# Forgetting attention and a SiLU feed-forward on one core: the mask of two late score groups on VectorE, DMA transposes issued ahead of loads, and the attention outputs of the fourth quad transposed by DMA

## The chip, the core and the metric

The kernel runs on one core of one Trainium2 chip. The metric is the device time of the core in microseconds (us). Before the change the median of 3 runs is 344.74 us, the lowest 343.42 and the highest 345.34. The profile that is shown is of one execution, with a span of 342.4 us.

## What is computed

Batch 8, heads 8, sequence 576, head dimension 64. Each head has causal attention with a decay that comes from running sums of log f. The result, 4608 rows of 512, goes through a feed-forward layer of width 2048 with SiLU.

```python
scores = np.matmul(q, k.transpose(0, 1, 3, 2)) / np.sqrt(D)
cum = np.cumsum(np.log(np.clip(f, 0.0001, 1.0)), axis=-1)
decay = cum[:, :, :, None] - cum[:, :, None, :]
scores = np.where(causal, -1e9, scores + decay)
attn = exp(scores - max) / (sum + 1e-9)
x = np.matmul(attn, v)            # (B, H, S, D), then to rows (B*S, H*D)
h = x @ w_in                      # 512 -> 2048
out = (h / (1 + np.exp(-h))) @ w_out
```

## The kernel before

**Decay.** The factor of a row cancels between numerator and sum, so only exp(-cum) of the key's position is left. It is multiplied into v (and into a column of ones beside v that gives the sum) on GpSimd: `convert_v0` (L340) for the first 128 positions of a batch, `convert_v` (L413) for the others.

**First section: the heads of all batches.** The first 128 positions of each batch are worked on alone. `turn0` (L277) turns q and k on TensorE, `scores0` (L309) makes the scores of the batch's 8 heads and ScalarE takes exp of them into u (L326). `out0` (L349) multiplies with v and VectorE normalises to xq (L368, L374); `back0` (L382) transposes xq on TensorE (L389) and ScalarE copies it to the feed-forward's input x (L390). The causal mask is made in one of two ways. `ban0` (L297) puts -30000 into the score bank with two 512-column matmuls of a ready-made ban (L300), and the scores are added on top. `mask0` (L333) leaves the bank alone and multiplies u with a triangle after exp, on VectorE (L335). Before the change batches 0 to 5 have the ban, 6 and 7 the mask. Batches 4 and 5 are done in the first call of `two_more` (L805), 6 and 7 in the second.

**Second section: the other 448 positions.** A *unit* n is a pair of heads of one batch, 32 in all; a *quad* m is two units, 16 in all, numbered from 0, so that the quad with m = 3 is the fourth. The loop over quads (L874) issues `scores`, `prepare` and `attend` of both units, and `back` of the quad before. `load_qk` (L152) loads q and k of a unit by four transfers from SyncE's queue (SP), `load_tails` (L165) and `load_v` (L174) use the same queue. `cast_qk` (L394) casts to bf16 on GpSimd, which works in program order and also issues the stores of the results (L591). `transposes` (L423) then turns q and k of the unit by a DMA transpose, again issued by SP. SP issues in program order: a transpose that waits for its cast holds all that stands behind it. `prepare(n)` (L839) casts and transposes unit n + 2 and loads unit n + 4.

`back(m)` (L531) transposes the normalised output xr of a quad to x. For the quads in `BY_DMA` (L488), 4 to 14 before the change, SP issues two DMA transposes (L538 for the 384 columns, L542 for the tail of 64 rows); for the others TensorE makes seven transposes (L548) and VectorE copies them out (L551, L554).

**Feed-forward, as filler.** The columns of x form groups: group 0 holds the heads of batches 0 to 3, 1 and 2 those of 4, 5 and of 6, 7, then one group of 384 columns for each batch (3 for batch 0, 4 for batch 1, and so on), and two groups of tails. `m1_chunk` (L560) makes one 128-row tile of h for a group: four matmuls (L567), tanh on ScalarE (L575), and gt on VectorE (L576). `m2_part` (L594) makes a quarter of an output tile: four matmuls (L612). Each such piece is called an M1 or M2 step here. `fill(us, least)` (L698) issues steps into the instruction order between pieces of attention, for an estimated number of microseconds and at least `least` steps; what is left or owed is carried in `at["left"]`. When no step can be issued, that is set to 0. `wanted` (L641) decides whether M1 or M2 is next, so that a group's M1 keeps pace with the M2 of the group before; a group's M1 may be issued once `ready` holds the group, and M2 once `open2` is set. In the loop a batch's group becomes ready two slots after `back` of its second quad. All of this is decided when the program is built; on the chip the order is fixed.

**Buffers.** Score banks: two of 2 PSUM banks (`psc`). All other PSUM tiles (hp, po, tp, tx, dn) share four banks in turn (`pbig`). th has three buffers, qkT three, qf and kf four.

Of the kernel before, what the change touches and what calls it, by code (L numbers as in the profile page):

```python
# [18 lines left out]
def kernel(  # L19
# [17 lines left out]
    NP = H // 2  # L37
# [7 lines left out]
    NU = B * NP  # L45
    NQ = NU // 2
# [52 lines left out]
    def xg(g):  # L99
        if g not in xgs:  # L100
            tag, bufs = {4 * P: ("x4", 1), 2 * P: ("x2" if g < 3 else "xt", 2), RB: ("x3", 3)}[GW[g]]
            xgs[g] = xpool.tile([P, NCC, GW[g]], BF16, name=tag, tag=tag, bufs=bufs)
        return xgs[g]
# [45 lines left out]
    def head(p, i):  # L149
        return p // 2 * 4 + 2 * i + p % 2  # L150

    def load_qk(n):  # L152
        b, p = divmod(n, NP)
        ts = []
        for name, src in (("qf", q), ("kf", k)):
            t = stage.tile([P, NR, 2, D], FP32, name=name, tag=name, bufs=4)
            for i in range(2):
                nc.sync.dma_start(
                    out=t[:, :, i, :],
                    in_=src[b, head(p, i), P:SM, :].rearrange("(c p) d -> p c d", p=P),  # L160
                )
            ts.append(t)
        qst[n] = tuple(ts)
# [113 lines left out]
    def turn0(b, i):  # L277
        src = qk0[b]
        if i == 0:
            qT0[b] = qktp.tile([P, NP, P], BF16, name="qT0", tag="qT0", bufs=2)  # L280
        dst, evac = ((qT0[b], nc.scalar.copy), (kT0[b], nc.vector.tensor_copy))[i]
        tp = pbig.tile([P, NP, NRUN, RUN], FP32, name="tp", tag="big")
        for c in range(RUN):
            for j in range(2):
                nc.tensor.matmul(  # L285
                    tp[j * D : (j + 1) * D, :, :, c].rearrange("p a r -> p (a r)"),
                    lhsT=src[:, i, c * D : (c + 1) * D],
                    rhs=sel[:, j, :],
                    start=True,
                    stop=True,  # L290
                )
        evac(
            out=dst[:, :, :].rearrange("p a t -> p (a t)"),
            in_=tp[:, :, :, :].rearrange("p a r c -> p (a r c)"),
        )

    def ban0(b):  # L297
        sc = psc.tile([P, 2, NP, P], FP32, name="sc", tag="sc")
        for i in range(2):
            nc.tensor.matmul(  # L300
                sc[:, i, :, :].rearrange("p a t -> p (a t)"),
                lhsT=ident_bf[:, :],
                rhs=ban[:, :, :].rearrange("p a t -> p (a t)"),
                start=True,
                stop=False,
            )
        return sc

    def scores0(b, sc=None):  # L309
        t = qT0.pop(b)  # L310
        fresh = sc is None
        u = upool.tile([P, 2, NP, P], BF16, name="u", tag="u")
        u0[b] = u
        if fresh:
            sc = psc.tile([P, 2, NP, P], FP32, name="sc", tag="sc")
        for p in range(NP):
            for i in range(2):
                r = slice(i * D, (i + 1) * D)
                nc.tensor.matmul(  # L319
                    sc[:, i, p, :],  # L320
                    lhsT=kT0[b][r, p, :],
                    rhs=t[r, p, :],
                    start=fresh,
                    stop=fresh or p == NP - 1,
                )
        nc.scalar.activation(  # L326
            out=u[:, :, :, :].rearrange("p i a t -> p (i a t)"),
            in_=sc[:, :, :, :].rearrange("p i a t -> p (i a t)"),
            func=ACT.Exp,
            scale=scale,  # L330
        )

    def mask0(b):  # L333
        x = u0[b][:, :, :, :].rearrange("p i a t -> p (i a) t")
        nc.vector.tensor_tensor(  # L335
            out=x, in0=x, in1=tri[:, None, :].to_broadcast([P, H, P]), op=ALU.mult
        )
# [85 lines left out]
    def transposes(n):  # L423
        src = qbf.pop(n)
        t = qktp.tile([P, NX, P], BF16, name="qkT", tag="qkT")
        qkT[n] = t[:, :, :].rearrange("p x c -> p (x c)")
        nc.sync.dma_start_transpose(
            out=t[:, :, :], in_=src[:, :, :].rearrange("p x c -> p (x c)")
        )
# [55 lines left out]

    NGR = 2 * NR + 1

    BY_DMA = [2 * 2 <= m < NQ - 1 for m in range(NQ)]  # L488

    def attend(n):  # L490
        b, p = divmod(n, NP)
# [39 lines left out]
    def back(m):  # L531
# [4 lines left out]
        xt = xg(g)[:, c0 : c0 + 2, :].rearrange("p i t -> p (i t)")[:, t0 * P : (t0 + 1) * P]  # L536
        if BY_DMA[m]:
            nc.sync.dma_start_transpose(  # L538
# [117 lines left out]
    def step(force=0):  # L656

        a, c = at["m1"], at["m2"]
        want = wanted(a, c)
        if not want:  # L660
            return None
        g1 = M1[a][0] if a < len(M1) else NG
        g2 = M2[c][0] if c < len(M2) else NG
        can1 = g1 in ready and not (M1[a][1] == 0 and g1 > g2 + 1)
        can2 = open2["w"] and c < len(M2) and g2 < g1
        kind = force if (force == 1 and can1) or (force == 2 and can2) else want
        if kind == 1:
            if M1[a][1] == 0:
                begin[g1] = (0, c)
            m1_chunk(g1, M1[a][1])  # L670
            at["m1"] += 1
            t = 4 * (GW[g1] / 2.4 + 2.5)
        else:
            m2_part(*M2[c])
            at["m2"] += 1
            t = 4 * (DM / 2.4 + 2.5)
        return t
# [6 lines left out]
    def plan(us_):  # L684

        a, c, kinds = at["m1"], at["m2"], []
        while us_ > 0:
            k = wanted(a, c)
            if not k:
                break  # L690
            kinds.append(k)
            if k == 1 and M1[a][1] == 0:
                begin[M1[a][0]] = (0, c)
            us_ -= (4 * (GW[M1[a][0]] / 2.4 + 2.5) if k == 1 else 4 * (DM / 2.4 + 2.5)) / 1000
            a, c = a + (k == 1), c + (k == 2)
        return kinds

    def fill(us_, least=0, ends=(0, 0)):  # L698

        left = us_ + at["left"]  # L700
        kinds = plan(left)
        kinds += [0] * (least - len(kinds))
        if any(ends) and kinds:
            if 2 not in kinds:
                kinds[0] = 2
            n1, n2 = len(kinds) - kinds.count(2), kinds.count(2)
            e0 = 1 if ends[0] else 0
            e1 = 1 if ends[1] and n2 > e0 else 0
            inner = n2 - e0 - e1
            n = n1 + inner  # L710
            mid = [2 if (x + 1) * inner // n > x * inner // n else 1 for x in range(n)]
            if inner and mid[-1] == 2 and e1 and not e0:
                mid = mid[::-1]
            kinds = [2] * e0 + mid + [2] * e1
        for k in kinds:
            t = step(k)
            if t is None:
                at["left"] = 0.0
                return
            left -= t / 1000  # L720
        at["left"] = left
# [80 lines left out]
    for c in range(NM):  # L802
        convert_v(0, c)

    def two_more(b, banned):  # L805
        for x in range(2):
            turn0(b + x, 0)
            turn0(b + x, 1)
            fill(0.6, 1)
        for x in range(2):  # L810
            if banned:
                scores0(b + x, ban0(b + x))
            else:
                scores0(b + x)
                mask0(b + x)
            fill(0.6 if x == 0 else 2.0 if banned else 2.8, 1 if x == 0 else 2)
        out0(b)
        fill(0.6, 1)
        out0(b + 1)
        fill(0.8, 2)  # L820
        back0(b, on_act)
        fill(0.6, 1)
        back0(b + 1, on_act)
        fill(0.6, 1)

    fill(5.0)
    two_more(4, True)
    ready.add(1)
    fill(5.0)
    open2["w"] = True  # L830
    begin[M1[at["m1"]][0]] = (M1[at["m1"]][1], at["m2"])
    fill(6.0)
    two_more(6, False)
    ready.add(2)
    fill(3.2)

    def prepare(n):  # L839

        b, p = divmod(n, NP)
        if n > NP - 1 and n + 4 < NU:
            load_qk(n + 4)
        if 0 < n < NU - 2:
            cast_qk(n + 2)
            transposes(n + 2)
        if n < NP - 1:
            load_qk(n + 4)
        if b + 1 == B:
            return  # L850
        if p == 0 and b > 0:
            load_tails(b + 1)
        if b == 0 and p >= 2 or b > 0 and p == 1:
            for c in range(NM) if b > 0 else range(2 * (p - 2), 2 * (p - 1)):
                load_v(b + 1, c)
        if n == NP - 1:
            load_qk(n + 4)
        if p >= 2:
            for c in range(2 * (p - 2), 2 * (p - 1)) if b > 0 else range(NM * (p - 2)):
                convert_v(b + 1, c)  # L860
# [13 lines left out]
    for m in range(NQ):  # L874
        n = 2 * m
# [4 lines left out]
        if m > 0:  # L880
            back(m - 1)
            if m % 2 == 0:
                b = m // 2 - 1
# [50 lines left out]
```

The softmax here doesn't subtract the row's maximum and nothing guards it: scores larger than these inputs give would overflow.

## Time and profile before

| | us | share of the span |
|---|---|---|
| span of the profiled execution | 342.4 | |
| TensorE, hp (L567), all shapes, 704 recorded | 128.3 | |
| TensorE, po (L612), 592 | 145.2 | |
| ScalarE busy | 216.6 | 63% |
| VectorE busy | 182.0 | 53% |
| GpSimd busy | 129.7 | 38% |
| chain that ended last: TensorE | | 91% |
| chain: ScalarE / VectorE / issue | | 5% / 3% / 1% |
| SP's queue: share of the 16 DMA engines' time | | 52.8% |

A line of a group or of the timeline gives start and length in us, engine, line of the kernel, operation, the tile that is written and those that are read (out<-in), shape and count; in brackets is the idle time of the engine just before it and what ended it. Matmuls overlap, so the length of a row of them is more than the time until the next one starts; the distance of starts is what TensorE spends. PE is the matmul, PEld the load of weights, DVE VectorE, ACT ScalarE, POOL GpSimd, SPq SyncE's issue of transfers. Some records of matmuls are missing, so a count can be too small.

### The profile page before, as it was taken

What the parts mean: (1) busy time and instruction counts of PE and PEld (TensorE: products, weight loads), DVE (VectorE), ACT (ScalarE), POOL (GpSimd) and SP (SyncE); (2) the same over time, 40 slices, a digit from 0 to 9 for tenths busy, and PEclk for the clock granted to TensorE, in tenths of its full rate; (3) what the DMA queues carried; (4) which work ended last, traced back from release to release, by engine and by line L of the source; (5) the groups of instructions that cost most, each with busy time, mean ns of one, the idle gap of its engine ahead of it and who ended that gap; (6) DMA issues with size and microseconds to landing.
All of it is one profiled execution on the core that took longest, in us unless ns stands there. A gap on an engine that the chain in (4) does not pass through costs nothing.

```text
span 342.4 us, 8894 instructions
## 1 busy us (share of the span) xinstructions
PE 335.9 (98%) x3567; PEld 199.2 (58%) x3567; DVE 182.0 (53%) x389; ACT 216.6 (63%) x401; POOL 129.7 (38%) x227
## 2 busy tenths in 40 slices
PE   8999999999999999999999999999999999999995
PEld 3745656577656656566465666656656565555654
DVE  4766736467557466357445654555655464444330
ACT  5767645877687676857759677595685944454431
POOL 8995317734637254065128128208320000001011
PEclk9999999999999999999999999999999999999999
DMA  8999999999999997899987799789832010001012
GB/s 154 193 183 220 179 202 155 241 212 199 197 192 179 189 198 168 164 215 162 162 195 153 162 192 214 159 148 218 166 86 56 25 42 33 31 32 63 31 53 71
DMA packets 141497, 50.44 MB, mean 147 GB/s; under 512 B 132368, under 2 KB 138768, under 8 KB 141456
## 3 DMA queue, kind: packets, MB, share of 16 engines
q1 hardware_dynamic: 131440, 32.70, 52.8%
q0 software_dynamic: 9856, 17.04, 21.3%
q8 instruction: 28, 0.46, 0.6%
q10 hardware_dynamic: 160, 0.13, 0.2%
q14 instruction: 13, 0.11, 0.1%
HBM read 36.85 MB, written 9.44 MB: 135 GB/s over the span
## 4 chain that ended last, share of the span: by engine, by line
PE 91%; ACT 5%; DVE 3%; issue 1%
PE po L612 36%; PE hp L567 34%; PE sc L459 7%; PE dn L506 5%; PE dn L515 3%; PE tp L285 3%; ACT u L463 2%; ACT th L575 2%; PE wm L232 1%; DVE gt L576 1%; PE sc L300 1%; PE sc L319 1%; ACT x L390 1%; DVE xq L374 0%; DVE xr L524 0%
## 5 line engine op out<-in xcount | busy, mean ns | idle before, releaser
L576 DVE SCALAR_TENSOR_TENSOR gt<-th,hp 128x384 bf16<-128x384 bf16 (+2 forms) x208 | 105.4, 522 | 82.9 <-ACT th L575 79.5
L575 ACT ACTIVATE th<-hp 128x384 bf16<-128x384 f32 (+2 forms) x208 | 95.2, 479 | 84.7 <-PE hp L567 82.5
L612 PE MATMUL po<-w_out_bf,gt 128*128 128x512 bf16 (+1 forms) x592 | 145.2, 374 | 0.0
L567 PE MATMUL hp<-x,w_in_bf 128*128 128x384 bf16 (+2 forms) x704 | 128.3, 321 | 0.6 <-DVE xt L554 0.4
L567 PEld LDWEIGHTS <-w_in_bf 128*128 128x128 bf16 x832 | 79.9, 98 | 57.0 <-DVE xt L554 0.7
L463 ACT ACTIVATE u<-sc 128x1024 bf16<-128x1024 f32 (+1 forms) x96 | 75.2, 821 | 9.7 <-PE sc L459 9.7
L612 PEld LDWEIGHTS <-gt 128*128 128x128 bf16 x592 | 53.3, 98 | 47.9 <-issue 2.5
L591 POOL DMA_DIRECT2D out_dram<-osb x38 | 21.0, 552 | 142.3 <-ACT osb L622 100.3
L413 POOL TENSOR_TENSOR vp<-vf,w_bf 128x520 bf16<-128x520 f32 (+1 forms) x32 | 35.2, 1104 | 27.7 <-DMA vf<-in_v_dram 26.2
L622 ACT ACTIVATE osb<-po 128x512 f32<-128x512 f32 (+1 forms) x37 | 22.1, 597 | 18.9 <-PE po L612 18.9
L468 DVE TENSOR_TENSOR u<-u,tri 128x768 bf16<-128x768 bf16 x32 | 21.6, 676 | 19.8 <-ACT u L463 19.8
L459 PE MATMUL sc<-qkT 64*128 64x128 bf16 (+1 forms) x640 | 26.7, 207 | 0.3 <-ACT th L575 0.2
L399 POOL CAST qkb<-qf 128x384 bf16<-128x384 f32 x32 | 17.4, 543 | 24.4 <-DMA qf<-in_q_dram 23.8
L482 DVE TENSOR_TENSOR ut<-ut,trit 128x128 bf16<-128x128 bf16 x32 | 9.5, 297 | 32.2 <-ACT ut L475 32.2
L459 PEld LDWEIGHTS <-qkT 64*128 64x128 bf16 x640 | 18.3, 94 | 11.7 <-issue 9.5
L475 ACT ACTIVATE ut<-sc 128x640 bf16<-128x640 f32 x32 | 23.3, 728 | 0.0
L506 PEld LDWEIGHTS <-u 128*128 128x128 bf16 x576 | 20.8, 97 | 2.5
L506 PE MATMUL dn<-vp,u 128*128 128x65 bf16 x384 | 21.8, 193 | 0.0
L524 DVE TENSOR_TENSOR xr<-dn,rec 128x448 bf16<-128x448 f32 x32 | 20.0, 625 | 1.1
L506 PE MATMUL dn<-v,u 128*128 128x65 bf16 x192 | 19.8, 193 | 0.0
L399 POOL CAST qkb<-kf 128x384 bf16<-128x384 f32 x32 | 16.9, 527 | 2.6 <-DMA kf<-in_k_dram 2.4
L567 PE MATMUL hp<-xt,w_in_bf 128*128 128x256 bf16 x128 | 17.7, 273 | 0.0
(68 smaller groups left out, 206.0 us busy)
## 6 DMA issues: line engine op xcount, KB each, us to landing
out_dram<-osb POOLq DMA_DIRECT2D x32, 256.0 KB, 3.2
vf<-in_v_dram SPq DMA_DIRECT2D x26, 256.0 KB, 5.2
qf<-in_q_dram SPq DMA_DIRECT2D x64, 96.0 KB, 3.3
kf<-in_k_dram SPq DMA_DIRECT2D x64, 96.0 KB, 2.9
w_in_bf<-in_moe_w_in_dram POOLq DMA_DIRECT2D x4, 512.0 KB, 7.2
w_out_bf<-in_moe_w_out_dram POOLq DMA_DIRECT2D x4, 512.0 KB, 10.1
vf<-in_v_dram POOLq DMA_DIRECT2D x6, 256.0 KB, 10.4
qkb<-in_q_dram POOLq DMA_DIRECT2D x8, 128.0 KB, 5.2
```

Source lines behind the costliest of these rows:

```text
L399: nc.gpsimd.tensor_copy(out=t2[:, c0 : c0 + NR, :].rearrange("p c x -> p (c x)"), in_=t[:, :, :, :].rearrange("p c h d -> p (c h d)"),)
L413: nc.gpsimd.tensor_tensor(out=vbf[b][r, c, :, :], in0=vst[b][c][r, :, :], in1=w_bf[r, c + 1, b * H : (b + 1) * H, None].to_broadcast([n, H ...
L459: nc.tensor.matmul(sc[:, i, o : o + q1 - q0], lhsT=kt, rhs=t[r, q0:q1], start=True, stop=True)
L463: nc.scalar.activation(out=u[:, :, c * SM : c * SM + w], in_=sc[:, :, 0:w], func=ACT.Exp, scale=scale)
L468: nc.vector.tensor_tensor(out=x, in0=x, in1=tri[:, None, None, :].to_broadcast([P, 2, NR, P]), op=ALU.mult,)
L475: nc.scalar.activation(out=ut[:, :, 0:3:2, :].rearrange("p k i t -> p i k t"), in_=sc[:, :, T0 : T0 + (NM + 1) * ST].rearrange("p i (k t) ...
L506: nc.tensor.matmul(dn[:, i * NR + c - 1, :], lhsT=u[:, i, o : o + P], rhs=vals(kb, i), start=(kb == 0), stop=(kb == c),)
L567: nc.tensor.matmul(hp[:, :], lhsT=w_in_bf[:, cc, fc * P : (fc + 1) * P], rhs=xcols(g, cc), start=(cc == 0), stop=(cc == NCC - 1),)
L575: nc.scalar.activation(out=th[:, :], in_=hp[:, :], func=ACT.Tanh, scale=0.5)
L576: nc.vector.scalar_tensor_tensor(out=gt[:, fc, :], in0=th[:, :], scalar=1.0, in1=hp[:, :], op0=ALU.add, op1=ALU.mult,)
L612: nc.tensor.matmul(po[:, :], lhsT=gt[:, fc, tb * P : (tb + 1) * P], rhs=w_out_bf[:, fc, m0:m1], start=(fc == 0), stop=(fc == NFC - 1),)
L622: nc.scalar.activation(out=osb[:, :], in_=po[:, :], func=ACT.Copy, scale=0.5)
```

## The change

Three things are changed. The scores of batches 4 and 5 get their mask from `mask0` on VectorE, as those of 6 and 7 do, instead of the ban's matmuls on TensorE; with that 0.8 us of filling is moved from the end of the first section to the place behind the scores of batches 4 and 5, where the mask has to be waited for. In `prepare` the cast and transpose of unit n + 2 now stand ahead of the loads of unit n + 4 in all units, where before that held only for n < 3. (For n = 3, the loads stay behind those of v.) And the quad with m = 3 is added to those that are transposed by DMA. The purpose is to take work off TensorE and to have transposed q and k earlier.

```diff
-    BY_DMA = [2 * 2 <= m < NQ - 1 for m in range(NQ)]
+    BY_DMA = [3 <= m < NQ - 1 for m in range(NQ)]
...
-    def two_more(b, banned):
+    def two_more(b):
         for x in range(2):
             turn0(b + x, 0)
             turn0(b + x, 1)
             fill(0.6, 1)
         for x in range(2):
-            if banned:
-                scores0(b + x, ban0(b + x))
-            else:
-                scores0(b + x)
-                mask0(b + x)
-            fill(0.6 if x == 0 else 2.0 if banned else 2.8, 1 if x == 0 else 2)
+            scores0(b + x)
+            mask0(b + x)
+            fill(0.6 if x == 0 else 2.8, 1 if x == 0 else 2)
         out0(b)
...
     fill(5.0)
-    two_more(4, True)
+    two_more(4)
     ready.add(1)
     fill(5.0)
     open2["w"] = True
     begin[M1[at["m1"]][0]] = (M1[at["m1"]][1], at["m2"])
     fill(6.0)
-    two_more(6, False)
+    two_more(6)
     ready.add(2)
-    fill(3.2)
+    fill(2.4)
...
     def prepare(n):
         b, p = divmod(n, NP)
-        if n > NP - 1 and n + 4 < NU:
-            load_qk(n + 4)
         if 0 < n < NU - 2:
             cast_qk(n + 2)
             transposes(n + 2)
-        if n < NP - 1:
+        if n != NP - 1 and n + 4 < NU:
             load_qk(n + 4)
```

## The prediction

> **What bounds the kernel now.** I read the page's first two parts, then the waits, then timelines of the stages that the change touches. A *step* below is four matmuls: an M1 step makes one hp tile (L567), an M2 step a quarter of a po tile (L612).
>
> The page, engine totals and the DMA row of the 40 slices:
>
> ```profile
> PE 335.9 (98%) x3567; PEld 199.2 (58%) x3567; DVE 182.0 (53%) x389; ACT 216.6 (63%) x401; POOL 129.7 (38%) x227
> ...
> DMA  8999999999999997899987799789832010001012
> ```
>
> TensorE is busy 98% of the span, and the starts of its matmuls confirm it: the 12 po from 140.20 end where the next ones start, 142.90, so 0.225 each with a change of shape, and 0.216 is the pitch elsewhere (36.11 to 36.98 is four). So each matmul removed is worth its pitch, and each wait of TensorE costs its length. The DMA row is at 7 to 9 up to slice 29: the transfers are close behind TensorE as a second limit.
>
> The end of the first section with heads by TensorE, on PE and then on ACT:
>
> ```profile
> 27.14 0.59 PE L300 MATMUL sc<-ban,ident_bf 128*128 128x512 bf16 x2
> 27.67 0.40 PE L319 MATMUL sc<-qT,kT 64*128 64x128 bf16 x8
> ...
> 34.79 1.03 PE L567 MATMUL hp<-x,w_in_bf 128*128 128x512 bf16 x4
> 35.89 0.38 PE L389 MATMUL tx<-ident_bf,xq 128*128 128x128 bf16 x4
> 36.11 3.90 PE L567 MATMUL hp<-x,w_in_bf 128*128 128x512 bf16 x28
> ```
>
> ```profile
> 35.85 0.60 ACT L575 ACTIVATE th<-hp 128x512 bf16<-128x512 f32 x1
> 36.35 0.58 ACT L390 COPY x<-tx 128x512 bf16<-128x512 bf16 x1
> ```
>
> To see: a ban costs 27.67 - 27.14 less the change of shape, about 0.43 for two matmuls; the copy of the last transpose ends at 36.93, 1.04 after that transpose began, and the 28 hp hide it, because their first four (0.87) belong to the old group. The same 28 take 36.11 to 39.85 = 3.74, where 4 x 0.216 + 24 x 0.109 = 3.48: 0.26 of waiting.
>
> The one quad's transposes on PE, and the weight load that waits for a DMA:
>
> ```profile
> 96.97 0.56 PE L548 MATMUL tx<-ident_bf,xr 128*128 128x128 bf16 x7
> 97.37 1.03 PE L612 MATMUL po<-w_out_bf,gt 128*128 128x512 bf16 x4
> ...
> 111.85 0.23 PEld L459 LDWEIGHTS <-qkT 64*128 64x128 bf16 x8 [0.35 <-DMA qkT<-qkb]
> ```
>
> Seven transposes hold PE 0.40. At 111.85 unit 9's scores waited 0.35 for their transposed q and k.
>
> SyncE's queue and what it waits for (SP, POOL, SP):
>
> ```profile
> 85.15 1.02 SPq L158 DMA_DIRECT2D kf<-in_k_dram  x2
> 88.45 1.25 SPq L427 DMA_TRANSPOSE qkT<-qkb  x1
> 89.74 0.62 SPq L168 DMA_DIRECT2D qktf<-in_q_dram  x1
> ...
> 88.13 0.29 POOL L403 CAST qkb<-qktf 128x128 bf16<-128x128 f32 x1
> ...
> 113.13 0.63 SPq L168 DMA_DIRECT2D qktf<-in_k_dram  x1
> ```
>
> To see: SP stood still from 86.17 to 88.45 for the cast that ended at 88.42, and after that issued nearly without a gap. It is the late one in this stage.
>
> **What the Trainium skill says.** "Perfetto Trace Analysis", Identifying the Most-Contended Engine: matmul busy share is not a measure of the distance from the limit; so I used starts, as above, and they agree that little is idle. "SBUF — State Buffer", SBUF: two separate sides: VectorE with two SBUF inputs and a GpSimd instruction that reads SBUF lock each other out. The trace agrees: the masks of L335 took 1.21 and 1.23 with GpSimd's L340 and casts beside them, while the smaller masks of L468 (128x768) range from 0.56 to 1.30. "DMA: Bandwidth & Descriptors", Anatomy of one DMA: about 2 us of a DMA are fixed, and a semaphore wait happens on the issuing sequencer, before dispatch. Both show here: the shortest landing of an x transpose is 2.8, and what stands behind a waiting transpose in SP's order is not issued.
>
> **The change, part by part.**
>
> *Mask in place of the ban, batches 4 and 5.* Removed: 4 matmuls of 512, 4 x 0.216 = **-0.86**. Added on DVE: two masks 128x1024. No fast one is in the trace: the lower bound is 0.75 (0.56 x 1024/768), the upper 1.23 (L335). GpSimd's converts of batches 4 and 5 run at 29.94 to 32.0, so I take 1.2. Between 27.14 and 35.9 DVE is busy 1.54 + 4.20 of 8.76; plus 2.4 it fits in sum, but in order the second mask stands ahead of three gt, and behind those are the two normalisations (L368, L374) that tx waits for, and the releases of hp buffers that PE waits for. out0(4) comes 2.6 after the scores in the new order (three steps), enough for the mask itself. I put **+0.3** (0 to 1.0).
>
> *The fill moved from the end to the first half.* The order of instructions shows an effect that the diff doesn't: one more step stands before out0(4), so group 0's M1 is used up when batch 5's tx is issued. `fill(0.6, 1)` finds nothing ready, sets what was owed to zero, and `fill(5.0)` runs 12 M1 steps of group 1 directly behind tx. Group 1 reads the x that this tx delivers. In the trace the copy ends 1.04 after tx begins, tx holds PE 0.22, and the semaphore takes some 0.05: **+0.85** of waiting (0.6 to 1.0) where now an old step hides it. Behind it wait all 12 steps and everything on PE. In that time DVE catches up, so the 0.26 in the 28 hp goes: **-0.26**.
>
> *Transposes of q and k ahead of loads.* From unit 4 each moves ahead of four loads (2.2 of issue), so unit 9's 0.35 goes: **-0.35**. But a transpose that waits for its cast now stops the loads behind it. At 84.08 SP issued four loads for unit 8 (2.09) under cover of that wait; after the change it stands from 84.08 to 88.45, and the 2.09 come later. Casts of later units have two units' time (some 14) from their loads, so I cost them at nothing.
>
> *Fourth quad by DMA.* Removed on PE: **-0.40**; on DVE two copies (0.55 and 0.21), hidden. Added: an x and an xt transpose, 1.24 of SP each, behind the tails of batch 3. Who waits: the third matmul of group 4's first M1 step. It starts at 116.28 + 2 x 0.163 = 116.6. Up to there the new order has two M2 steps more (1.73) and lacks ban and tx (1.26): +0.47; with +0.85 + 0.3 - 0.26 - 0.35 it is at 117.6. The tails' issue ends at 113.77; with the 2.09, none recovered, 115.9; all recovered, [...] 113.8. I take the middle, 114.8. Landing: median 4.3 on the page (2.8 to 5.9 in the trace). So x is there at 119.1: **+1.5** (0 to 4.2). The next even quad shows how close this is. Landings of its xt and x, and PE:
>
> ```profile
> DMA to landing us min/median/max: 5.0/5.4/5.9
> ...
> 144.30 1.21 PE L567 MATMUL hp<-x,w_in_bf 128*128 128x384 bf16 x6
> ```
>
> x was issued at 138.72 and landed 5.9 later, 144.6, just when the third matmul of group 5 starts (144.30 + 0.33). SP is there 1.1 behind the scores of its quad (136.2, tails at 137.32); at the fourth quad's x it is 4.2 behind (108.23, tails at 112.46). The later quads' x is safe: PE is later by then.
>
> Sum: -0.86 - 0.40 - 0.35 - 0.26 + 0.3 + 0.85 + 1.5 = **+0.8**: 345.5.
>
> **Rivals.** (1) *x comes in time*: SP makes up the lost issue, or x lands in 2.8 (113.8 + 2.8 = 116.6). Then +0.8 - 1.5 = -0.7: 344.0. For it: earlier transposes relieve SP's queue of nothing but order, yet vf loads took 4.23 for four, which is pressure and may shrink. Against: quad 6's margin of nothing. (2) *No new wait*: masks lie in DVE's idle time and ACT's copy is done sooner; 344.74 - 0.86 - 0.40 - 0.35 - 0.26 = 342.9, faster by 0.5%. Against: the order puts dependent hp right behind tx. (3) *Transfers become the bound*: nothing recovered and landing 5.9, so +4.2, DVE +1.0: 344.74 - 1.26 - 0.61 + 0.85 + 1.0 + 4.2 = 348.9; half of that excess over the forecast gives 347.2, slower. For it: the DMA row at 9. Against: from 126.91 on SP itself waited for DVE (L538 11.4 in all), so it catches up.
>
> **Numbers.** Forecast 345.5: 0.45. Rival 1: 0.22. Rival 2: 0.15. Rival 3: 0.18. The bound of 0.5% is 1.72: 343.0 to 346.5. Rival 2 and a little of rival 1 are faster: 0.2; rival 3 and the upper part of the forecast slower: 0.25; the rest 0.55. The range runs from just under rival 2 to just over rival 3's half way, 342.7 to 347.4.
>
> **What would show it.** A wait of PE of 0.6 to 1.0 at its first 256-column hp, for ACT's x; no L300 after 20; no wait for qkT near 112; SP idle from about 84 to 88 with unit 8's loads after it; and a wait of PE at some 117 to 119 for DMA x. If the last is missing, rival 1 holds; if the first is too, rival 2. If SP falls behind in several quads, with PE waiting for qkT or x after 140, the prediction is wrong on the upper side.

## The result and the profile after

The changed kernel takes 349.39 us (median of 4 runs, 348.04 to 350.43) where the kernel before took 344.88 in the same session: a ratio of 1.0136, 95% interval 1.009 to 1.0182. It is slower by 1.4%, outside the predicted range. The profiled spans are 347.6 and 342.4.

The page after, engine totals, clock and the chain of waits:

```profile
PE 330.6 (95%) x3509; PEld 198.5 (57%) x3556; DVE 181.9 (52%) x389; ACT 217.5 (63%) x401; POOL 129.4 (37%) x227
...
PEclk9999999999999899999999999999999999999999
...
PE 60%; DMA 20%; SPq 8%; POOL 6%; issue 4%; ACT 1%; DVE 0%; POOLq 0%; ACTq 0%
```

TensorE's busy time is 5.3 us less in a span that is 5.2 us longer. This difference is no measure of the loss: part of it is the work that was removed, and part are records that this trace lacks (550 of the 592 po matmuls are in it). So what follows goes by the starts of matmuls and by the waits. One slice of the clock is down to 8. And the chain, 91% TensorE before, now runs through transfers, SyncE's queue and GpSimd for 34% of the span. The waits of TensorE, longest first:

```profile
PE hp L567 <- DMA x<-xr: 4.4, 2, 3.0
...
PE hp L567 <- ACT x L390: 0.7, 1, 0.7
```

The two waits for x on PE's timeline. The x is that of the fourth quad (m = 3) in the first and of the sixth (m = 5) in the second; each falls into the next round of the loop, m = 4 and m = 6, where `back` of m - 1 stands:

```profile
117.10 0.49 PE L567 MATMUL hp<-x,w_in_bf 128*128 128x384 bf16 x2
120.58 0.80 PE L567 MATMUL hp<-x,w_in_bf 128*128 128x384 bf16 x2 [2.99 <-DMA x<-xr]
...
147.84 0.49 PE L567 MATMUL hp<-x,w_in_bf 128*128 128x384 bf16 x2
149.75 0.97 PE L567 MATMUL hp<-x,w_in_bf 128*128 128x384 bf16 x5 [1.42 <-DMA x<-xr]
```

In both the first two matmuls of a step run (their columns of x are there) and the third stops. It was due 2 x 0.163 after the first, at 117.43 and 148.17, and started 3.15 and 1.58 later. "The first wait" and "the second wait" below are these two.

How x came to be late, on the chain in order of time (start, length, what), with the start of SyncE's share and its end:

```profile
88.34 0.25 POOL qkb L403
88.60 1.25 SPq L427
89.85 0.04 issue
89.89 0.58 SPq L158
...
114.84 0.63 SPq L168
115.48 0.05 issue
115.58 4.96 DMA x<-xr
120.58 0.48 PE hp L567
```

SyncE waits for a cast until 88.6, issues the transpose, and only then the loads of unit 8 (89.89). From there the chain goes on without a long stop, through SyncE's issues, landings of loads and GpSimd's casts, up to x's issue at 115.58 and its landing at 120.54.

What came during and after the first wait, engines by microsecond (columns: stretch, length, busy of PE, PEld, DVE, ACT, POOL with counts, clock, share of the DMA engines, GB/s):

```profile
118.00:119.00 1.00, 0.00 (x0) 0.00 (x0) 0.23 (x1) 0.03 (x1) 0.12 (x1) 1.00 0.82 148
119.00:120.00 1.00, 0.00 (x0) 0.00 (x0) 0.00 (x0) 0.00 (x0) 0.17 (x1) 0.95 0.60 144
120.00:121.00 1.00, 0.42 (x2) 0.25 (x2) 0.00 (x0) 0.00 (x0) 0.00 (x0) 0.50 1.10 206
121.00:122.00 1.00, 1.00 (x5) 0.45 (x4) 0.06 (x1) 0.49 (x1) 0.00 (x0) 0.50 0.53 119
122.00:123.00 1.00, 1.00 (x13) 0.69 (x11) 0.49 (x1) 0.30 (x1) 0.00 (x0) 0.50 0.87 196
123.00:124.00 1.00, 1.00 (x32) 1.00 (x30) 0.66 (x2) 0.19 (x1) 0.00 (x0) 0.84 0.63 143
```

The clock falls to half just before 120 and stays there until about 123.3. After the work resumes at 120.58 each microsecond of it loses what the clock is short of 1: 0.42 x 0.5 + 0.5 + 0.5 + 0.16 = 1.37.

And the end of the first section, on PE:

```profile
35.82 0.38 PE L389 MATMUL tx<-ident_bf,xq 128*128 128x128 bf16 x4
36.91 5.40 PE L567 MATMUL hp<-x,w_in_bf 128*128 128x256 bf16 x48 [0.70 <-ACT x L390]
```

The twelve dependent steps stand right behind tx; the first starts 0.87 after the 36.04 at which tx was through. The sum closes: 3.15 + 1.37 + 1.58 + 0.87 = 6.97 lost, less the 1.87 that the prediction counted as removed (ban 0.86, tx 0.40, unit 9's wait 0.35, the 0.26 in the 28 hp; none of these is in the trace any more), is 5.1, against 5.2 between the spans of this one pair of executions. Between the medians it is 4.5.

### The profile page after: what moved, and what is told of

Same layout as the page of the kernel before. It is cut to its first block, busy times and chain, and to the rows that moved or that the text cites. A ratio compares the mean times of both kernels' runs of the same rounds, so it can differ in the third digit from the quotient of the medians.

```text
span 347.6 us, 8829 instructions
## 1 busy us (share of the span) xinstructions
PE 330.6 (95%) x3509; PEld 198.5 (57%) x3556; DVE 181.9 (52%) x389; ACT 217.5 (63%) x401; POOL 129.4 (37%) x227
## 4 chain that ended last, share of the span: by engine, by line
PE 60%; DMA 20%; SPq 8%; POOL 6%; issue 4%; ACT 1%; DVE 0%; POOLq 0%; ACTq 0%
PE po L612 25%; PE hp L567 24%; DMA kf<-in_k_dram 6%; PE sc L459 4%; DMA vf<-in_v_dram 4%; PE dn L506 4%; SPq L158 4%; DMA x<-xr 3%; DMA w_out_bf<-in_moe_w_out_dram 3%; PE dn L515 2%; SPq L427 2%; DMA qkb<-in_k_dram 1%; SPq L179 1%; POOL qkb L399 1%; DMA qf<-in_q_dram 1%
## 5 line engine op out<-in xcount | busy, mean ns | idle before, releaser
L612 PE MATMUL po<-w_out_bf,gt 128*128 128x512 bf16 (+1 forms) x550 | 138.1, 373 | 3.7 <-issue 2.2
L413 POOL TENSOR_TENSOR vp<-vf,w_bf 128x520 bf16<-128x520 f32 (+1 forms) x32 | 34.4, 1081 | 38.3 <-DMA vf<-in_v_dram 28.0
L399 POOL CAST qkb<-qf 128x384 bf16<-128x384 f32 x32 | 16.7, 521 | 30.0 <-DMA qf<-in_q_dram 28.2
L399 POOL CAST qkb<-kf 128x384 bf16<-128x384 f32 x32 | 17.8, 555 | 6.7 <-DMA kf<-in_k_dram 6.7
```

Of the source, the lines that this page charges most:

```text
L399: nc.gpsimd.tensor_copy(out=t2[:, c0 : c0 + NR, :].rearrange("p c x -> p (c x)"), in_=t[:, :, :, :].rearrange("p c h d -> p (c h d)"),)
L413: nc.gpsimd.tensor_tensor(out=vbf[b][r, c, :, :], in0=vst[b][c][r, :, :], in1=w_bf[r, c + 1, b * H : (b + 1) * H, None].to_broadcast([n, H ...
L612: nc.tensor.matmul(po[:, :], lhsT=gt[:, fc, tb * P : (tb + 1) * P], rhs=w_out_bf[:, fc, m0:m1], start=(fc == 0), stop=(fc == NFC - 1),)
```

## Experiments

The first question was which of the three parts does it. Theory 1: the waits for x, from the fourth quad and the order. Theory 2: the order by itself. Theory 3: the mask with its moved fill. Ratios are to the kernel before, with 95% intervals.

### The mask alone

```diff
-    two_more(4, True)
+    two_more(4, False)
...
-    fill(3.2)
+    fill(2.4)
```

> Only the mask of batches 4 and 5 and the moved fill; loads ahead of transposes and the fourth quad on TensorE as before. Theory 1 (the loss is the wait for x by DMA in the fourth and sixth quads): the ban's -0.86 is given back by the copy that TensorE waits for (+0.7 to +0.87), so within 0.7 us of before, 344.2 to 345.6, and no wait for a DMA at the first 384-column hp of group 4. Theory 3 (the step order that the fill makes is what costs): slower by 2 us or more, with TensorE waiting for ScalarE or VectorE in many places.

Measured 345.20, ratio 0.9994 (0.9972 to 1.0016). The wait for ScalarE's copy is there (0.8), and only 0.2 of waiting for x, in the sixth quad. Theory 3 falls. What was not expected: in the profiled execution, the slowest of its 14, the scores of unit 3 waited for qkT.

```profile
PE sc L459 <- DMA qkT<-qkb: 2.0, 1, 2.0
```

TensorE was there before the transpose had landed. That this comes of the step order is not shown: the traces of the changed kernel and of five kernels below have the same mask and fills and no such wait, and two kernels with the ban show a short one at unit 3 (0.13 with the fourth quad alone, 0.34 with order and fourth quad).

### The order alone

```diff
-        if n > NP - 1 and n + 4 < NU:
-            load_qk(n + 4)
         if 0 < n < NU - 2:
             cast_qk(n + 2)
             transposes(n + 2)
-        if n < NP - 1:
+        if n != NP - 1 and n + 4 < NU:
             load_qk(n + 4)
```

> Only cast and transpose ahead of the loads. Theory 1: unit 9's wait of 0.35 goes; the loads of unit 8 and all behind them are issued some 2 us later, and where x by DMA had no margin (sixth quad: landed 144.65, needed 144.63) TensorE waits 0.5 to 1.5 us; together 0 to +1.2, 344.9 to 346.1. Theory 2 (the order alone makes SyncE's queue late in several quads): +2 us or more, 347 and up, waits for x in more than two quads. If the order is harmless: -0.35.

Measured 345.61, ratio 0.9988 (0.9964 to 1.0013): no difference. Unit 9's wait is gone and one short wait for x, at the step that had no margin, has come. Theory 2 falls.

```profile
143.37 0.49 PE L567 MATMUL hp<-x,w_in_bf 128*128 128x384 bf16 x2
144.12 0.97 PE L567 MATMUL hp<-x,w_in_bf 128*128 128x384 bf16 x5 [0.27 <-DMA x<-xr]
```

### The fourth quad alone

```diff
-    BY_DMA = [2 * 2 <= m < NQ - 1 for m in range(NQ)]
+    BY_DMA = [3 <= m < NQ - 1 for m in range(NQ)]
```

> Only the fourth quad's x by DMA, with loads ahead of transposes as before. SyncE's tails are issued by 113.8 there, so x is issued 113.8 and lands 118.2 to 119.7 (4.4 to 5.9); it is needed at about 116.2 (116.28 + 0.33 - 0.40). Theory 1: a wait of 2.0 to 3.5 us[...]: +1.5 to +4.5, 346.4 to 349.4. Theory 2: without the new order there is hardly a wait, 344.0 to 345.0.

Measured 345.94, ratio 0.9998 (0.9973 to 1.0022). This is where theory 1 missed: SyncE issued x when expected, but it landed 3.24 later, at 117.32, and the step, due at 117.14, waited only 0.2. TensorE was there 0.9 later than expected, for it had waited 1.06 before, for unit 9's qkT. SyncE and PE:

```profile
113.35 0.63 SPq L168 DMA_DIRECT2D qktf<-in_k_dram  x1
114.08 1.27 SPq L538 DMA_TRANSPOSE x<-xr  x1
...
112.38 0.40 PE L459 MATMUL sc<-qkT 64*128 64x128 bf16 x8 [1.06 <-DMA qkT<-qkb]
...
116.81 1.69 PE L567 MATMUL hp<-x,w_in_bf 128*128 128x384 bf16 x8
```

So none of the three parts alone costs anything that these runs resolve; the intervals end at 1.0022 or lower. The loss needs at least two of them.

### All but the fourth quad

```diff
-    BY_DMA = [3 <= m < NQ - 1 for m in range(NQ)]
+    BY_DMA = [2 * 2 <= m < NQ - 1 for m in range(NQ)]
```

> The changed kernel with the fourth quad on TensorE again (mask and order kept). Theory 1: the wait of 3.16 us and the lower clock behind it go, +0.40 comes back; x of the sixth quad then finds TensorE earlier by the 4 to 5 us that the fourth's wait had given, so its wait of 1.6 grows to 2 to 4 us: 345.5 to 348. If the sixth quad's lateness came from the fourth quad's two extra transposes (2.5 us of SyncE), it is gone and the time is 344.0 to 344.8.

Measured 345.76, ratio 1.0015 (0.9994 to 1.0036). Two waits for x are left:

```profile
PE hp L567 <- DMA x<-xr: 1.5, 2, 1.2
```

The larger is the second wait, 1.37 by the starts against 1.58 in the changed kernel. It neither grew, as theory 1 had it, nor went, so it does not need the fourth quad's own transposes. With the fourth quad's x on TensorE the first wait and the half clock are gone, and nearly all of the loss with them.

### Order and fourth quad, with the ban

The changed kernel with `two_more(4, True)`, the ban and the old fills:

> The changed kernel with the ban for batches 4 and 5 (order and fourth quad kept). Theory A (order and fourth quad together make x late: the order puts the issue of x some 1.5 us later than without it, the quad makes TensorE wait for it): PE waits 2.5 to 3.5 us at group 4's first step, its clock drops after, and the time is 347.5 to 349.5. Theory B (the mask's other step order is needed too): a wait under 1.5 us, no drop of the clock, 345 to 346.5.

Measured 349.46, ratio 1.0096 (1.0072 to 1.0121). Theory A holds: order and quad are enough. SyncE issues x even later here, since it had stood for unit 6's cast until 89.83 (88.60 in the changed kernel). Unit 9's scores waited 0.8 for qkT in this execution, though its transpose stands ahead of the loads. SyncE and PE of this kernel:

```profile
117.32 1.28 SPq L538 DMA_TRANSPOSE x<-xr  x1
...
120.62 1.46 PE L567 MATMUL hp<-x,w_in_bf 128*128 128x384 bf16 x6 [3.42 <-DMA x<-xr]
```

### Mask and fourth quad, with loads first

The changed kernel with `prepare` as before:

> The changed kernel with loads ahead of transposes again (mask and fourth quad kept). Theory A: x of the fourth quad is issued about 114 and lands by 118.5; unit 4's qkT is late by 2 us as in the run with the mask alone, which pushes TensorE back, so the wait for x is under 1 us and the time 344.5 to 346.5. Theory B (mask and quad are what costs, the order not): 348 or more.

Measured 345.63, ratio 0.9994 (0.9967 to 1.0021), x issued at 114.22. The fourth quad's x is waited for by nobody, and the sixth's for 1.18 by the starts:

```profile
114.22 1.27 SPq L538 DMA_TRANSPOSE x<-xr  x1
...
117.16 1.46 PE L567 MATMUL hp<-x,w_in_bf 128*128 128x384 bf16 x8
...
143.46 0.49 PE L567 MATMUL hp<-x,w_in_bf 128*128 128x384 bf16 x2
144.97 1.14 PE L567 MATMUL hp<-x,w_in_bf 128*128 128x384 bf16 x6 [1.03 <-DMA x<-xr]
```

Theory A holds, though not by the wait for qkT that I expected (it was unit 3's in the run with the mask alone): in this execution there was none. The fourth quad's x is issued at 114.1 to 114.2 with loads first and at 115.6 to 117.3 with transposes first, whatever the mask. The second wait is there with loads first too, so it is not the order alone that makes it.

### One unit's loads put back

If the order makes x late because SyncE stands idle from 85 to 88.6 for the cast, then it is enough to let unit 8's loads use that time.

```diff
+        if n == NP:
+            load_qk(n + 4)
         if 0 < n < NU - 2:
             cast_qk(n + 2)
             transposes(n + 2)
-        if n != NP - 1 and n + 4 < NU:
+        if n not in (NP - 1, NP) and n + 4 < NU:
             load_qk(n + 4)
```

> The changed kernel with one exception: the loads of unit 8 stand ahead of unit 6's transpose, as before. If the 2.09 us of issue that SyncE lost while it stood waiting for the cast at 84 to 88 is what made x late, x is issued 1.5 to 2.1 us earlier than in the changed kernel (113.5 to 114.5), the wait for x is 0.5 to 2 us, the clock does not drop, and the time is 344.5 to 347. If the lateness gathers over all units (each transpose ahead of its loads costs a little), x is issued within 0.7 us of 115.6 and the time stays over 347.5.

Measured 346.03, ratio 1.0009 (0.9986 to 1.0031). SyncE, and PE at the two steps:

```profile
85.98 1.02 SPq L158 DMA_DIRECT2D kf<-in_k_dram  x2
88.63 1.25 SPq L427 DMA_TRANSPOSE qkT<-qkb  x1
...
114.06 1.28 SPq L538 DMA_TRANSPOSE x<-xr  x1
...
117.02 1.46 PE L567 MATMUL hp<-x,w_in_bf 128*128 128x384 bf16 x8
...
145.77 0.97 PE L567 MATMUL hp<-x,w_in_bf 128*128 128x384 bf16 x5 [1.70 <-DMA x<-xr]
```

One unit's four loads, moved by one place, bring x's issue from 115.58 to 114.06. The eight hp from 117.02 run without a stop: the first wait, of which 0.5 to 2 us were expected to stay, is gone, and the clock stays full. Only 1.5 of the 3.2 by which x is there earlier are the issue, though; the rest is a landing of 3.25 instead of 4.96. In the other two kernels that keep the changed order for unit 8 and for x (the one with the ban, and the one with work in the wait, below) the issue was later still, at 117.32 and 117.02, and the landings took 3.25 and 3.44. x was there at 120.5 to 120.6 in all three, and at 117.3 to 117.4 in the three kernels that issue unit 8's loads first. The second wait is still there, 1.86 by the starts.

### x ahead of everything else

```diff
+        if m > 0 and BY_DMA[m - 1]:
+            back(m - 1)
         prepare(n)
         if m > 0:
-            back(m - 1)
+            if not BY_DMA[m - 1]:
+                back(m - 1)
```

> The changed kernel, but a quad's x transposes are issued ahead of the next unit's qkT transpose, loads and tails. If the lateness of x on SyncE's queue is the cause, x of the fourth quad is issued at 108 to 112 and landed by 117, TensorE waits for no x and its clock stays: 343.5 to 345. If the transfers' own speed is the cause (too many bytes for the 16 engines), the late ones are now others, qkT or loads, and the time stays over 346.5.

Measured 344.83, ratio 0.9991 (0.9971 to 1.001).

```profile
110.97 1.21 SPq L538 DMA_TRANSPOSE x<-xr  x1
...
116.96 1.30 PE L567 MATMUL hp<-x,w_in_bf 128*128 128x384 bf16 x7
```

All bytes and all instructions of the changed kernel are there, only x stands 4.6 us earlier in SyncE's queue, and no step waits for x. So it was the place in the queue, not the amount of transfers.

### Work in the first wait

```diff
+        if g == 4 and fc == 0:
+            keep_warm(12)
         hp = pbig.tile([P, w], FP32, name="hp", tag="big")
```

> The changed kernel with 12 matmuls on zeros (512 columns, result unused) issued just before group 4's first step, so that TensorE works through most of its wait for x (12 x 0.216 = 2.6 us). x lands when it did, so the wait's end stays near 120.5. If the half clock from 120 to 123.4 comes of the idle stretch, it is gone and the time is 1.5 to 2 us less than the changed kernel's 349.4, so 347.4 to 347.9. If it has another cause, the clock drops all the same and the time is 349 to 349.8.

Measured 348.11, ratio 1.0062 (1.004 to 1.0084), clear of the changed kernel's interval, though the gain is a little less than expected. PE (two lines were added, so hp stands in L569), and in the next fence the stretch with its clock:

```profile
116.76 2.75 PE L232 MATMUL wm<-warm 128*128 128x512 bf16 x12
119.35 0.49 PE L569 MATMUL hp<-x,w_in_bf 128*128 128x384 bf16 x2
120.50 1.14 PE L569 MATMUL hp<-x,w_in_bf 128*128 128x384 bf16 x6 [0.66 <-DMA x<-xr]
```

```profile
118.00:124.00 6.00, 5.29 (x75) 3.46 (x74) 2.50 (x7) 0.98 (x2) 0.42 (x2) 1.00 0.94 135
```

The third matmul starts at 120.50, as late as before (120.58), and the clock stays at 1.00. It is not this one execution alone: the granted clock over the whole span is 0.994 or 0.995 in all four executions of the changed kernel, which is what one drop to half for 3.4 us makes (1.7 of 347.6), and 0.998 or more in 19 of the 20 of this one. So the half clock came of the idle stretch, and was a cost of its own. By the medians it is 1.3 us (1.35 against the kernel with the ban, measured beside this one), near the 1.37 of the trace; by the ratios it is 2.6, with intervals wide enough for both, and the second wait was also shorter in this execution (0.74).

### x first, and an old step behind tx

The kernel with x first, and the fill of batches 4 and 5 back at 2.0:

```diff
-            fill(0.6 if x == 0 else 2.8, 1 if x == 0 else 2)
+            fill(0.6 if x == 0 else 2.0 if b == 4 else 2.8, 1 if x == 0 else 2)
...
-    fill(2.4)
+    fill(3.2)
```

> The kernel with x transposes first on SyncE's queue, and with the fill behind the scores of batches 4 and 5 at 2.0 and the last one at 3.2 again, so that one step of group 0 stands behind batch 5's tx. If the copy that TensorE waited for (0.7 to 0.87) is what the moved fill cost, PE has no wait for L390 any more, and the time is 0.6 to 0.9 below the run with x first alone: 0.4% to 0.8% faster than before. If the mask then delays out0(4), a wait for VectorE or for u takes its place and nothing is gained.

Measured 345.08, ratio 0.9978 (0.9957 to 1.0). PE at the end of the first section:

```profile
35.57 0.38 PE L389 MATMUL tx<-ident_bf,xq 128*128 128x128 bf16 x4
35.79 3.91 PE L567 MATMUL hp<-x,w_in_bf 128*128 128x512 bf16 x28
```

The wait for the copy is gone: the 512-column step hides it, as it did before the change. But the 28 take 3.74 again (the next matmul starts at 39.53), so the 0.26 of waiting in them, gone in the changed kernel, is back. The gain is less than expected, 0.2% against 0.4 to 0.8, and its interval touches no difference. Against x first alone (0.9991) it can't be told apart. It is the best of the kernels tried, by a margin that these runs do not settle.

## Why the prediction was wrong

It forecast 345.5 in a range of 342.7 to 347.4; it is 349.4. The wait for the fourth quad's x was named and taken at half its size; the wait for the sixth quad's x was put at nothing; and TensorE's clock had no term.

- **What is removed.** Right. All four terms, 1.87, are gone from the trace; what each was worth alone was not measured.
- **The moved fill.** Right: 0.85 forecast, 0.87 measured.
- **The mask on VectorE.** +0.3 forecast; no wait of TensorE for a mask or a gt shows in that stage beyond the one at tx that was there before. One of the two masks took 0.69, less than the lower bound of 0.75, the other 1.22, beside GpSimd's L340.
- **Transposes ahead of loads.** The loss of 2.09 of issue was forecast, and the run with unit 8's loads put back shows it as the cause: 1.5 us of issue come back. Unit 9's wait is gone in the changed kernel, as forecast; with the ban beside the same order it is there again, at 0.8, so that part is not safe.
- **The first wait: the step that failed in size.** "I take the middle, 114.8. Landing: median 4.3." SyncE made up nearly nothing: x was issued at 115.58, by the upper end of 115.9, which is 0.78 later than the middle. The landing was 4.96, 0.66 longer. TensorE was there at 117.43, where 117.6 was forecast. So the term was 3.15 instead of 1.5. The prediction itself had read that SP issued nearly without a gap after 88.45, and that was a reason to take the upper end of the issue.
- **"The later quads' x is safe: PE is later by then": wrong.** The term in the sum was nothing, and it measured 1.58. x for the sixth quad's step was issued at 142.72, landed 6.99 later at 149.70 and was needed at 148.17. TensorE was there 3.54 later than before the change (144.63), but SyncE issued 4.00 later (138.72), and the landing took 6.99 instead of 5.93. So some 0.5 of the wait is the shift and 1.1 the longer landing. The prediction had shown a margin of nothing at this very step, and gave it no room for either. The same step waited in other kernels too: 0.42 with the order alone, 0.36 with the fourth quad alone, 1.18 with mask and fourth quad, 1.86 with unit 8 put back. A wait for x after 140 was among the prediction's own signs of being wrong on the upper side, and it came.
- **Not in the sum at all: TensorE's clock after a long wait**, 1.37.

1.65 + 1.58 + 1.37 = 4.6 is missing from the forecast sum of +0.8; less the 0.3 for the mask that did not come, that makes 5.1, near the difference of the spans. Rival 3, with 348.9 at its end and 347.2 as its time, had one thing right, that hardly any of the lost issue is recovered. That its 348.9 lies so near is luck: it has 4.2 for the wait and 1.0 for VectorE, which measured 3.15 and nothing, and neither the second wait nor the clock. And the transfers were not the bound: x first moves the same bytes in 344.8.

The prediction had quoted the Trainium skill ("DMA: Bandwidth & Descriptors", Anatomy of one DMA) for a semaphore wait happening on the issuing sequencer, before dispatch, and the traces agree: in the changed kernel SyncE issues nothing between 85.18 and 88.60, where the transpose waits for its cast. What I did not draw from it is that such a wait delays everything later in the queue until the queue next has slack, and here there was hardly any before 115.

What stays open: why a landing takes 3.2 in some executions and 5 to 7 in others. In both long ones of the changed kernel GpSimd issued an output store some 0.25 us after x. In the twelve traces together 4 of the 140 x transposes have a store that close behind them (0.24 to 0.28); they landed after 4.97, 6.64, 6.99 and 7.38, and none of the other 136 took as long as 6. But no run moves a store alone, so this is a pattern and not a shown cause. As the second wait is mostly such a landing, its cause stays open with it. Why unit 3's scores waited 2.0 for qkT in one execution and not at all in most others was not followed either.

## What to carry to other kernels

In a queue that issues in order and has little slack, putting an instruction that waits ahead of ones that don't delays all of these, and the bill comes at whichever consumer has the least margin. Here four loads that take 2.09 to issue were put behind such a wait, and a transfer 27 us further down the queue was still issued 1.5 us late. So before such a swap, list the margins of all consumers down the queue (landing against need), and add the shift and the spread of the landings to each of them. Where the consumer is nearest, issue its transfer first: x ahead of loads that nobody needs for 14 us cost nothing and took all the waits for x away. And a change of fill should be checked for what now stands directly behind the producer.

## What the runs showed of the hardware that I had not expected

TensorE's clock fell to half after a wait of 3 us in the middle of a kernel that was otherwise at full clock, and stayed there for 3.4 us in both profiled executions where that happened (idle for 2.99 and 3.42), most of that after the work had resumed. Shorter waits left it at full: 1.42 in the same profile, 1.70 with unit 8's loads put back, 2.00 with the mask alone. The Trainium skill ("TensorE: Matmul & The Clock Gate", What's actually happening) describes a free-running activity window of about 3.4 us that sets the clock. The length of the drop agrees, 3.4 in both; in the changed kernel the wait that brought it about, 2.99, was shorter than the window.
